# Sparse attention and a gated feed-forward on one core: another hand-written order of all steps

## The chip, the core and the metric

The kernel runs on one core of a Trainium2 chip. A core has five engines that work at the same time, each through its own queue in program order: PE (matrix products), DVE (vector), ACT (activation functions), POOL (general) and SP (which here only starts transfers). Sixteen DMA engines move data. The metric is the device time of one execution in microseconds. A profile records one execution on the same core.

## The reference

```python
# q, k, v: (4, 8, 768, 64): batch, heads, positions, head dimension
k_sum = k in blocks of 32 positions, maximum over the block       # 24 blocks
v_sum = v in blocks of 32 positions, mean over the block
scores_l = q @ k.T / 8, kept where |position difference| < 16
scores_s = q @ k_sum.T / 8 + log(32)
a = softmax(concat(scores_l, scores_s))
attn = a @ concat(v, v_sum)                                       # (4, 8, 768, 64)
x = attn.transpose(0, 2, 1, 3).reshape(3072, 512)
h = x @ w_in                                                      # (3072, 2048)
out = (h / (1 + exp(-beta * h))) @ w_out                          # (3072, 512)
```

## The kernel before, in words

The four batches go through the same stages, one after another on PE: the attention of batch b, then the products with w_in ("h", 16 column tiles of 128 by 768 tokens), then the products with w_out ("o", 6 tiles of 128 tokens by 512, each in 4 parts). Only the attention of batch 0 stands alone, ahead of everything. The attention of batch b+1 is woven into the o stage of batch b and partly into its h stage.

Attention works by head pairs: two of the eight heads, four pairs for each batch. The order of every step on every engine is written out by hand: the string ORDER (L528 to L585) is walked once (the loop at L637), and each word emits the instructions of one step into the queues of the engines concerned. A word is step.batch.pair, with a letter at the end where the engine is chosen by hand: P is POOL, D is DVE, A is ACT, S is the transfer queue of SP. A plus sign ahead of a step takes its PSUM buffer from the tag "big" (three buffers) and not from "t" (two). The steps of a pair are:

- ld.k, ld.q, ld.v load 384 KB each. They are started on SP, in the order of the string (L92, L103). Batch 0 goes to buffers of its own, later batches share five "hold" buffers.
- kc, qc cast k and q to bf16 (L98 in batches 0 and 1). kt, qt transpose them on PE (L257), ke, qe copy the result out of PSUM (L267, L272, L276).
- km takes the block maxima of k on DVE (L296), ks spreads them into the windows (L302, L303).
- vc0, vc1 cast v (L322; in later batches POOL casts the whole, and DVE's vr sorts the rows), vd makes the shifted copy of its rows (L327 and L328 as transfers, L331 and L332 as copies), vm forms the block means on PE (L347), ve takes them out (L355, L356, or L358 when they are not split in two halves), vs spreads them (L366 as a copy, L363 as a transfer).
- s0, s1 are the scores on PE. With the letter P the mask is added on PE (L395, L397) ahead of the scores (L403); later batches have L413. e0, e1 are the exponentials on ACT (L420), m0, m1 the masks on DVE (L426).
- a0, a1 are the products with v on PE (L442), n0, n1 the division by the row sums on DVE (L449, L450).
- x transposes the pair's output on PE (L462) and xe copies it out (L466). x0, x1, xe0, xe1 are halves of these. xx does the whole by one transposing transfer from SP instead (L469).

The h products of one tile (L485) contract over the four head pairs. hp does the first three pairs of a tile, hq the fourth, so that hp can start before the last pair is ready. hs is the Silu on ACT (L490). The products with w_out are at L510, their copies out of PSUM at L516 (oe), the stores at L522 (os).

The weights are loaded by POOL's queue, cast on the way: w_in in three parts wa (column tiles 0 to 3), wb (4 to 9), wc (10 to 15), w_out in two, wd (row tiles 0 to 7) and we (8 to 15). A dictionary AFTER makes some loads wait for the landing of another, to keep the transfers in a chosen order; a wait stands in the queue of the issuing engine, so what is queued behind it waits as well. ws.n (L202) divides row tile n of w_out by beta on DVE. cz, cy, cw are constants for later batches, te and tl load ACT's tables for exponential and Silu. fp.n issues n products with a buffer of zeros (L232), whose result nobody reads.

Of the kernel before, what the change touches and what calls it, by code (L numbers as in the profile page):

```python
# [11 lines left out]
def kernel(  # L12
# [505 lines left out]
    def o_store(b, ms, eng, c=slice(0, d_model)):  # L518
# [7 lines left out]


    ORDER = (  # L528
        "wm.0 sp.2 fp.14 ci.0 ld.k.0.3S on.0 ld.k.0.2S cb.0 cm.0 ld.q.0.0S lb.0 ld.v.0.0S ld.v.0.1S sp.0 "
        "ld.k.0.0S ct.0 sp.1 sp.3 ld.q.0.2S kc.0.3D ld.v.0.2S bt.0 +kt.0.3 kc.0.2A ld.v.0.3S ke.0.3D qc.0.0P "  # L530
        "ld.q.0.1S fp.3 +kt.0.2 km.0.3 ld.k.0.1S ke.0.2A fp.1 +qt.0.0 ks.0.3P qe.0.0A km.0.2 ld.q.0.3S vc1.0.0P "
        "vc0.0.0D ks.0.2P fp.6 vm.0.0 vc0.0.1A vc1.0.1P vd.0.0S ve.0.0 vd.0.1P vm.0.1P kc.0.0A ve.0.1 vs.0.0A "
        "vs.0.1D fp.2 kt.0.0 ke.0.0D qc.0.2A km.0.0 vc1.0.2P fp.6 qt.0.2 ks.0.0D qe.0.2A vc0.0.2D fp.1 s0.0.0P wa "
        "vc0.0.3A vd.0.2D s0.0.2P vc1.0.3P e0.0.0 qc.0.1D vm.0.2P wb s1.0.2P vd.0.3S e0.0.2 ve.0.2 kc.0.1D "
        "+qt.0.1 e1.0.2 +vm.0.3P wc vs.0.2D kt.0.1 s1.0.0P ke.0.1A qe.0.1D wd e1.0.0 we km.0.1 fp.1 +a0.0.0 "
        "qc.0.3P a1.0.0 n0.0.0 ks.0.1P qt.0.3 n1.0.0 ve.0.3 fp.1 x.0.0 vs.0.3D s0.0.1P qe.0.3D +a0.0.2 e0.0.1 "
        "+a1.0.2 n0.0.2 s1.0.1P n1.0.2 +a0.0.1 e1.0.1 xe.0.0D x.0.2 s1.0.3P xe.0.2A n0.0.1 +a1.0.1 e1.0.3 n1.0.1 "
# [12 lines left out]
        "qe.1.3A a1.1.0 os.0.1 o.0.2.1 kc.2.0 n0.1.1 vd.1.3S o.0.2.2 n1.1.0 kx.2.0 s1.1.2 km.1.3 xx.1.0 s0.1.2 "  # L550
        "e1.1.2 ld.v.2.1S a1.1.1 o.0.2.3 ks.1.3P n1.1.1 e0.1.2 qc.2.0 s0.1.3 m1.1.2 oe.0.2A o.0.3.0 xx.1.1 m0.1.2 "
        "e0.1.3 a1.1.2 a0.1.2 vc.2.0 n1.1.2 s1.1.3 o.0.3.1 os.0.2 e1.1.3 n0.1.2 vm.2.0 vr.2.0 tl.1 o.0.3.2 kc.2.1 "
        "ve.2.0 xx.1.2 vm.1.3 o.0.3.3 vs.2.0D o.0.4.0 qc.2.1 m1.1.3 ld.k.2.2S oe.0.3A ve.1.3 kx.2.1 o.0.4.1 "
        "m0.1.3 os.0.3 o.0.4.2 vs.1.3D vd.2.0S o.0.4.3 ke.2.0A km.2.0 a0.1.3 oe.0.4D a1.1.3 o.0.5.0 ld.q.2.2S "
        "n0.1.3 o.0.5.1 ks.2.0D os.0.4 vc.2.1 n1.1.3 x0.1.3 o.0.5.2 xe0.1.3A vr.2.1 ld.v.2.2S x1.1.3 vm.2.1 "
        "o.0.5.3 xe1.1.3D ld.k.2.3S ve.2.1 h.1.0 oe.0.5D vs.2.1D os.0.5 h.1.1 hs.1.0 vd.2.1D ld.q.2.3S kc.2.2 "
        "h.1.2 hs.1.1 km.2.1 kx.2.2 ke.2.1A h.1.3 ld.v.2.3S hs.1.2 ks.2.1D h.1.4 hs.1.3 qx.2.0 h.1.5 hs.1.4 "
        "qx.2.1 h.1.6 hs.1.5 h.1.7 hs.1.6 vc.2.2 h.1.8 hs.1.7 vr.2.2 vm.2.2 hs.1.8 h.1.9 kc.2.3 vd.2.2D ve.2.2 "
        "kx.2.3 h.1.10 hs.1.9 vs.2.2D h.1.11 hs.1.10 h.1.12 hs.1.11 km.2.2 ke.2.2A h.1.13 hs.1.12 ks.2.2D vc.2.3 "
        "h.1.14 hs.1.13 qc.2.2 vr.2.3 vm.2.3 hs.1.14 h.1.15 vd.2.3S ve.2.3 vs.2.3D qc.2.3 qx.2.2 ld.k.3.0S s1.2.0 "  # L560
        "hs.1.15 ld.q.3.0S s0.2.0 o.1.0.0 qx.2.3 ld.v.3.0S te.2 s0.2.1 ld.k.3.1S km.2.3 o.1.0.1 ld.q.3.1S e0.2.0 "
        "ke.2.3D o.1.0.2 ks.2.3D e1.2.0 o.1.0.3 m0.2.0 e0.2.1 m1.2.0 o.1.1.0 oe.1.0A m0.2.1 a0.2.0 os.1.0 s1.2.1 "
        "n0.2.0 a1.2.0 e1.2.1 o.1.1.1 n1.2.0 kc.3.0 s0.2.2 m1.2.1 xx.2.0 a0.2.1 e0.2.2 ld.v.3.1S s1.2.2 n0.2.1 "
        "o.1.1.2 kx.3.0 e1.2.2 qc.3.0 m0.2.2 a1.2.1 m1.2.2 o.1.1.3 ld.k.3.2S n1.2.1 a0.2.2 s1.2.3 oe.1.1D s0.2.3 "
        "xx.2.1 e1.2.3 o.1.2.0 n0.2.2 e0.2.3 m1.2.3 o.1.2.1 vc.3.0 tl.2 os.1.1 m0.2.3 a1.2.3 a1.2.2 vr.3.0 a0.2.3 "
        "kc.3.1 o.1.2.2 n1.2.2 vd.3.0S o.1.2.3 n1.2.3 o.1.3.0 qc.3.1 n0.2.3 xx.2.2 vm.3.0 oe.1.2D o.1.3.1 xx.2.3 "
        "ve.3.0 o.1.3.2 vs.3.0D o.1.3.3 os.1.2 o.1.4.0 oe.1.3A qx.3.1 vc.3.1 o.1.4.1 ke.3.0A km.3.0 vm.3.1 "
        "o.1.4.2 os.1.3 vr.3.1 o.1.4.3 qx.3.0 kc.3.2 vd.3.1D o.1.5.0 ks.3.0D kx.3.2 o.1.5.1 ld.q.3.2S oe.1.4D "
        "o.1.5.2 ve.3.1 os.1.4 vs.3.1D o.1.5.3 ld.v.3.2S h.2.0 oe.1.5D kx.3.1 h.2.1 hs.2.0 h.2.2 hs.2.1 os.1.5 "
        "h.2.3 hs.2.2 ld.k.3.3S h.2.4 hs.2.3 ld.q.3.3S h.2.5 hs.2.4 ld.v.3.3S h.2.6 hs.2.5 km.3.2 h.2.7 hs.2.6 "  # L570
        "ke.3.2D ks.3.2D qc.3.2 h.2.8 hs.2.7 qx.3.2 h.2.9 hs.2.8 h.2.10 hs.2.9 vc.3.2 h.2.11 hs.2.10 km.3.1 "
        "vr.3.2 vm.3.2 hs.2.11 h.2.12 vd.3.2D h.2.13 ve.3.2 hs.2.12 kc.3.3 vs.3.2D h.2.14 ke.3.1D hs.2.13 kx.3.3 "
        "ks.3.1D qc.3.3 h.2.15 hs.2.14 qx.3.3 s0.3.0 hs.2.15 s0.3.1 vc.3.3 o.2.0.0 te.3 vr.3.3 vm.3.3 o.2.0.1 "
        "vd.3.3D e0.3.1 o.2.0.2 ve.3.3 ke.3.3A o.2.0.3 vs.3.3D e0.3.0 o.2.1.0 m0.3.1 oe.2.0A km.3.3 a0.3.1 s1.3.2 "
        "os.2.0 s1.3.0 n0.3.1 e1.3.2 o.2.1.1 ks.3.3D e1.3.0 o.2.1.2 m1.3.2 m1.3.0 a1.3.2 o.2.1.3 m0.3.0 n1.3.2 "
        "a1.3.0 oe.2.1A a0.3.0 n1.3.0 o.2.2.0 os.2.1 n0.3.0 s1.3.1 s0.3.2 e1.3.1 xx.3.0 o.2.2.1 e0.3.2 m1.3.1 "
        "o.2.2.2 m0.3.2 a1.3.1 s0.3.3 n1.3.1 a0.3.2 e0.3.3 o.2.2.3 n0.3.2 xx.3.1 s1.3.3 m0.3.3 xx.3.2 o.2.3.0 "
        "e1.3.3 oe.2.2D a0.3.3 tl.3 m1.3.3 os.2.2 o.2.3.1 n0.3.3 a1.3.3 o.2.3.2 n1.3.3 o.2.3.3 xx.3.3 o.2.4.0 "
        "oe.2.3D o.2.4.1 os.2.3 o.2.4.2 o.2.4.3 o.2.5.0 oe.2.4D o.2.5.1 os.2.4 o.2.5.2 o.2.5.3 h.3.0 oe.2.5A "
        "os.2.5 h.3.1 hs.3.0 h.3.2 hs.3.1 h.3.3 hs.3.2 h.3.4 hs.3.3 h.3.5 hs.3.4 h.3.6 hs.3.5 h.3.7 hs.3.6 h.3.8 "  # L580
        "hs.3.7 h.3.9 hs.3.8 h.3.10 hs.3.9 h.3.11 hs.3.10 h.3.12 hs.3.11 h.3.13 hs.3.12 h.3.14 hs.3.13 h.3.15 "
        "hs.3.14 o.3.0.0 hs.3.15 o.3.0.1 o.3.0.2 o.3.0.3 o.3.1.0 oe.3.0A o.3.1.1 os.3.0 o.3.1.2 o.3.1.3 o.3.2.0 "
        "oe.3.1D o.3.2.1 os.3.1 o.3.2.2 o.3.2.3 o.3.3.0 oe.3.2D o.3.3.1 os.3.2 o.3.3.2 o.3.3.3 o.3.4.0 oe.3.3D "
        "o.3.4.1 os.3.3 o.3.4.2 o.3.4.3 o.3.5.0 oe.3.4A o.3.5.1 oe0.3.5 os0.3.5 os.3.4 o.3.5.2 o.3.5.3 oe1.3.5 "
        "os1.3.5 ")  # L585
# [102 lines left out]
```

## Time and profile before

| | |
|---|---|
| median of 6 runs | 231.34 us (230.16 to 234.21) |
| the profiled execution | 231.34 us |
| its span, from first to last instruction | 229.3 us |
| outside the span | 2.0 us |
| instructions | 4653 |
| busy, PE / DVE / ACT / POOL | 216.6 / 128.0 / 121.5 / 49.9 us |
| granted TensorE clock | 0.998 |
| transfers | 37.47 MB; read from HBM 27.27 MB |

The page gives busy time by engine, a map of the span in slices, the transfers, the chain of work that ended last and the costliest groups of instructions. The trace can also be asked for stretches of time, for one engine in order of time, and for waits. PE ends are modelled: a busy PE is not always a PE at its peak.

### The profile page before, as it was taken

To read this page: it belongs to the slowest core of one execution; us is meant where nothing else is said; L and a number is where in the kernel's file an instruction comes from. 1 tells how busy PE (TensorE), PEld (TensorE's weight loads), DVE (VectorE), ACT (ScalarE), POOL (GpSimd) and SP (SyncE) were. 2 spreads that over 40 slices of the span, in tenths; PEclk is the share of its full clock that TensorE was granted. 3 is DMA by queue.
4 is the path that set the end of the run, shared out by engine and by line. 5 is a ranking of instruction groups with operands and counts; after the bars stand their busy time and mean duration, and the time that the engine had idled before them with its cause. 6 is when DMAs were issued, how large, how long until landed. Compare 5 with 4: busy or idle time off the path is not lost.

```text
span 229.3 us, 4653 instructions
## 1 busy us (share of the span) xinstructions
PE 216.6 (94%) x1880; PEld 122.5 (53%) x1880; DVE 128.0 (56%) x298; ACT 121.5 (53%) x151; POOL 49.9 (22%) x76
## 2 busy tenths in 40 slices
PE   7777799999899999999999999999999999999992
PEld 3535565666456455556564455655454456654462
DVE  7789978697998976344689642353766100001111
ACT  2586276678777605667844216768554067661010
POOL 0587001250864320340243200240000000000000
PEclk9999999999999999999999999999999999999999
DMA  6999999993999799993999999993126210001212
GB/s 192 274 305 243 210 198 235 237 256 86 241 218 245 157 252 227 256 177 63 218 232 202 175 230 224 243 176 68 49 80 140 103 46 0 3 1 46 93 46 93
DMA packets 89510, 37.47 MB, mean 163 GB/s; under 512 B 78816, under 2 KB 84720, under 8 KB 89488
## 3 DMA queue, kind: packets, MB, share of 16 engines
q1 hardware_dynamic: 85728, 32.94, 64.2%
q0 software_dynamic: 3664, 4.19, 10.8%
q8 instruction: 14, 0.23, 0.4%
q14 instruction: 8, 0.07, 0.1%
q10 hardware_dynamic: 96, 0.04, 0.1%
HBM read 27.27 MB, written 6.29 MB: 146 GB/s over the span
## 4 chain that ended last, share of the span: by engine, by line
PE 83%; DVE 9%; DMA 3%; POOL 1%; issue 1%; ACT 1%; SPq 1%; DVEq 0%; ACTq 0%; POOLq 0%
PE h_ps L485 37%; PE o_ps L510 35%; PE s_ps L413 4%; PE av_ps L442 3%; DMA room_v<-in_v_dram 3%; PE vm_ps L347 2%; DVE attn L426 1%; DVE km L296 1%; DVE vt L366 1%; DVE kw L267 1%; PE px L462 1%; DVE x_nat L450 1%; POOL vt L322 1%; ACT attn L420 1%; DVE run L98 1%
## 5 line engine op out<-in xcount | busy, mean ns | idle before, releaser
L510 PE MATMUL o_ps<-w_out_sb,h_sb 128*128 128x512 bf16 (+1 forms) x400 | 88.8, 371 | 0.0
L485 PE MATMUL h_ps<-xT,w_in_sb 128*128 128x384 bf16 x512 | 85.0, 326 | 0.1
L490 ACT ACTIVATE h_sb<-h_ps,beta_sb 128x768 bf16<-128x768 f32 x64 | 57.3, 900 | 35.9 <-PE h_ps L485 35.3
L485 PEld LDWEIGHTS <-w_in_sb 128*128 128x128 bf16 x512 | 49.6, 98 | 33.1 <-issue 0.3
L510 PEld LDWEIGHTS <-h_sb 128*128 128x128 bf16 x400 | 36.7, 98 | 37.2
L516 DVE COPY o_sb<-o_ps 128x512 f32<-128x512 f32 (+1 forms) x14 | 9.1, 652 | 49.9 <-PE o_ps L510 49.8
L420 ACT ACTIVATE attn<-s_ps 128x768 bf16<-128x768 f32 x32 | 25.0, 807 | 16.6 <-PE s_ps L413 10.7
L516 ACT COPY o_sb<-o_ps 128x512 f32<-128x512 f32 x11 | 6.4, 586 | 33.3 <-PE o_ps L510 33.1
L426 DVE TENSOR_TENSOR attn<-attn,band 128x768 bf16<-128x768 bf16 x24 | 16.6, 703 | 4.5 <-ACT attn L420 3.5
L450 DVE TENSOR_TENSOR x_nat<-av_ps,r 128x384 bf16<-128x384 f32 x32 | 17.8, 558 | 1.1
L316 POOL CAST v_nat<-hold_n 128x768 bf16<-128x768 f32 x12 | 10.8, 899 | 23.0 <-DMA hold_n<-in_v_dram 15.6
L442 PEld LDWEIGHTS <-attn 128*64 128x64 bf16 x384 | 8.3, 110 | 7.9 <-issue 5.2
L248 POOL CAST qz<-hold_n 128x384 bf16<-128x384 f32 x16 | 8.4, 555 | 17.8 <-DMA hold_n<-in_q_dram 16.3
L296 DVE TENSOR_REDUCE km<-kT 128x24 bf16<-128x768 bf16 x8 | 7.6, 952 | 8.0 <-DMA kT<-k_nat 7.8
L232 PE MATMUL fill<-filler 128*128 128x384 bf16 x37 | 10.1, 403 | 2.0 <-DVE filler L636 1.2
L355 DVE COPY part<-vm_ps 32x128 f32<-32x128 f32 x15 | 4.4, 296 | 13.3 <-PE vm_ps L347 12.9
L322 DVE COPY vt<-v_nat 64x768 bf16<-64x768 bf16 x24 | 10.2, 426 | 2.4 <-POOL v_nat L316 2.2
L242 POOL CAST k_nat<-hold_n 128x768 bf16<-128x768 f32 x8 | 7.0, 880 | 19.6 <-DMA hold_n<-in_k_dram 19.1
L98 POOL CAST run<-hold_n 96x1024 bf16<-96x1024 f32 (+1 forms) x8 | 8.0, 1010 | 14.6 <-DMA hold_n<-in_k_dram 14.6
L413 PE MATMUL s_ps<-q,kw 128*128 128x128 bf16 (+2 forms) x156 | 11.0, 215 | 0.1
L442 PE MATMUL av_ps<-vt,attn 128*64 128x65 bf16 x384 | 10.8, 198 | 0.2
L128 ACT ACT_TABLE_LOAD x8 | 10.3, 1283 | 0.9 <-PEq L672 0.7
(88 smaller groups left out, 165.9 us busy)
## 6 DMA issues: line engine op xcount, KB each, us to landing
out_dram<-o_sb SPq DMA_DIRECT2D x20, 256.0 KB, 2.4
hold_n<-in_k_dram SPq DMA_DIRECT2D x12, 384.0 KB, 5.3
hold_n<-in_q_dram SPq DMA_DIRECT2D x12, 384.0 KB, 5.6
hold_n<-in_v_dram SPq DMA_DIRECT2D x12, 384.0 KB, 4.5
w_out_sb<-in_moe_w_out_dram POOLq DMA_DIRECT2D x2, 1024.0 KB, 19.3
room_k<-in_k_dram SPq DMA_DIRECT2D x4, 384.0 KB, 4.5
room_q<-in_q_dram SPq DMA_DIRECT2D x4, 384.0 KB, 5.5
room_v<-in_v_dram SPq DMA_DIRECT2D x4, 384.0 KB, 6.2
```

Of the source, the lines that this page charges most:

```text
L128: nc.scalar.activation(out=warm[:, 1:2], in_=warm[:, 0:1], func=func)
L316: nc.gpsimd.tensor_copy(out=t.rearrange("p c h d -> p h c d"), in_=f.rearrange("p (h c d) -> p h c d", h=2, d=D))
L322: copy(out=vdst(vt(b, g))[0:QT, par::2], in_=src[par * QT:(par + 1) * QT])
L413: nc.tensor.matmul(sv[:, i // NH, i % NH, :, lo:hi], window(kw, t), q2_bufs[g][:, :, t0:t0 + hi - lo], start=True, stop=True)
L420: nc.scalar.activation(out=dst, in_=src, func=ACTF.Exp, scale=scale)
L426: nc.vector.tensor_mul(out=a, in0=a, in1=band[:, u * nch:(u + 1) * nch, None].to_broadcast([P, nch, 2, QT]))
L442: nc.tensor.matmul(o[par * QT:(par + 1) * QT, mi * VW + c.start:mi * VW + c.stop], a[:, i, h] if b else a[:, h, i], v_t[:, u * nch + i, c] ...
L450: nc.vector.tensor_mul(out=x[:, u * NH:(u + 1) * NH], in0=ov.rearrange("p m (h e) -> p m h e", e=VH)[:, :, :, 0:D], in1=r[:, :, :, None].t ...
L485: nc.tensor.matmul(big[:, kk, 0:MG], w_in_sb[:, ki, ni * P:(ni + 1) * P], xT[b][:, ki, kk * MG:(kk + 1) * MG], start=(ki == 0), stop=(ki = ...
L490: nc.scalar.activation(out=h_bufs[(b, ni // 8)][:, ni % 8, :].rearrange("p (k m) -> p k m", k=2), in_=h_open[(b, ni)][:, :, 0:MG], func=AC ...
L510: nc.tensor.matmul(o_ps[(b, ms)][:, c], h_bufs[(b, ni // 8)][:, ni % 8, ms * P:(ms + 1) * P], w_out_sb[:, ni, c], start=(ni == 0), stop=(n ...
L516: copy(out=o_out[(b, ms)][:, c], in_=o_ps[(b, ms)][:, c])
```

## The change

The kernel's functions stay as they are. ORDER and AFTER are replaced. What differs most:

- Batch 0: the pairs are loaded and computed in the order 1, 0, 2, 3 (before: k of pair 3 and 2, then q and v of pair 0, then mixed, with k and q of pair 1 and 3 last).
- Batch 0: several steps have another engine. All ke and qe are on ACT (two of each were on DVE). vs is on POOL twice and a transfer once (before: three times DVE, once ACT). xe of pair 1 is replaced by the transposing transfer xx.0.1. kc of one pair is on POOL. ks of pairs 0 and 1 is on DVE. Three vm are not split.
- 25 filler products in place of 37.
- wa waits for q of pair 3 (before: v of pair 3). In batch 1, k and q of pair 0 wait for wc, and v of pair 0 for wd; k of pair 1 no longer waits for we.
- Batch 1: the first three h tiles are begun on three of the four pairs (hp.1.0 to hp.1.2, hq.1.0 to hq.1.2) in place of h.1.0 to h.1.2. So it was done in batch 0 already.
- Steps of batches 1 to 3 change places by a few words and some change their engine.

The core of the diff (the lines up to the first products with w_in, the start of h in batch 1, and AFTER):

```diff
-        "wm.0 sp.2 fp.14 ci.0 ld.k.0.3S on.0 ld.k.0.2S cb.0 cm.0 ld.q.0.0S lb.0 ld.v.0.0S ld.v.0.1S sp.0 "
-        "ld.k.0.0S ct.0 sp.1 sp.3 ld.q.0.2S kc.0.3D ld.v.0.2S bt.0 +kt.0.3 kc.0.2A ld.v.0.3S ke.0.3D qc.0.0P "
-        "ld.q.0.1S fp.3 +kt.0.2 km.0.3 ld.k.0.1S ke.0.2A fp.1 +qt.0.0 ks.0.3P qe.0.0A km.0.2 ld.q.0.3S vc1.0.0P "
...
+        "wm.0 sp.0 fp.14 ci.0 ld.k.0.1S sp.2 sp.1 sp.3 cb.0 ld.v.0.1S cm.0 ld.k.0.0S lb.0 ld.q.0.1S ld.v.0.0S "
+        "on.0 ld.v.0.2S ct.0 ld.q.0.0S kc.0.1D ld.k.0.2S bt.0 kt.0.1 ke.0.1A vc0.0.1P ld.k.0.3S vc1.0.1A km.0.1 "
+        "ld.v.0.3S kc.0.0A fp.6 +vm.0.1 vd.0.1P ks.0.1D ld.q.0.2S ld.q.0.3S qc.0.1A ve.0.1 +kt.0.0 ke.0.0A "
+        "vs.0.1P qt.0.1 vc1.0.0D vc0.0.0A km.0.0 qe.0.1A fp.3 vm.0.0P vd.0.0S vc0.0.2P ks.0.0D s0.0.1P ve.0.0 "
+        "s1.0.1P vc1.0.2D qc.0.0P e0.0.1 +vm.0.2 vd.0.2S vs.0.0P e1.0.1 +qt.0.0 ve.0.2 kc.0.2A a0.0.1 vs.0.2S "
+        "+a1.0.1 kc.0.3P n0.0.1 qe.0.0A +kt.0.2 n1.0.1 kt.0.3 ke.0.2A s1.0.0P vc1.0.3P vc0.0.3D xx.0.1 ke.0.3A "
+        "s0.0.0P km.0.2 qc.0.2P e1.0.0 vm.0.3 km.0.3 ks.0.2P e0.0.0 +qt.0.2 wa a1.0.0 ve.0.3 qe.0.2A qc.0.3D "
+        "a0.0.0 ks.0.3P n1.0.0 +qt.0.3 s1.0.2P wb qe.0.3A vd.0.3D s0.0.2P wc e1.0.2 n0.0.0 s1.0.3P wd e0.0.2 "
+        "vs.0.3D +a1.0.2 we e1.0.3 x.0.0 n1.0.2 +a0.0.2 xe.0.0A s0.0.3P n0.0.2 +a1.0.3 e0.0.3 x.0.2 n1.0.3 tl.0 "
+        "fp.1 a0.0.3 xe.0.2D +x1.0.3 n0.0.3 fp.1 hp.0.0 xe1.0.3A x0.0.3 hp.0.1 xe0.0.3A hq.0.0 hq.0.1 hs.0.0 "
...
+        "ws.4 ld.k.1.1S ws.7 ke.1.0A ld.q.1.1S ws.5 qc.1.0P h.0.11 ws.3 ld.v.1.1S hs.0.10 km.1.0 qt.1.0 ws.0 "
+        "hs.0.11 h.0.12 ws.2 ws.1 qe.1.0A ks.1.0D h.0.13 hs.0.12 h.0.14 ws.11 ld.k.1.2S ws.10 hs.0.13 ws.14 "
+        "h.0.15 ws.13 hs.0.14 ws.15 ws.9 vc.1.0 s0.1.0 ws.8 hs.0.15 s1.1.0 ws.12 ld.q.1.2S vm.1.0 vr.1.0 kc.1.1P "
...
-        "o.0.5.3 xe1.1.3D ld.k.2.3S ve.2.1 h.1.0 oe.0.5D vs.2.1D os.0.5 h.1.1 hs.1.0 vd.2.1D ld.q.2.3S kc.2.2 "
+        "xe0.1.3A x1.1.3 ks.2.0D vm.2.0 oe.0.5A ld.k.2.3S hp.1.0 vc.2.1 xe1.1.3D ve.2.0 hq.1.0 vs.2.0D vm.2.1 "
+        "hs.1.0 hp.1.1 os.0.5 vr.2.1 hq.1.1 hp.1.2 kc.2.2 ve.2.1 ld.q.2.3S hs.1.1 vs.2.1D hq.1.2 kx.2.2 h.1.3 "
...
-    AFTER = {"wa": "ld.v.0.3", "wb": "ld.q.0.2", "wc": "ld.q.0.3", "wd": "ld.q.0.3", "we": "ld.q.0.3", "ld.k.1.0": "wc", "ld.q.1.0": "wd", "ld.v.1.0": "wb", "ld.k.1.1": "we", "ld.q.1.1": "wb", "ld.v.1.1": "wc", "ld.k.1.2": "wd", "ld.q.1.2": "wb", "ld.v.1.2": "we", "ld.q.1.3": "wc", "ld.v.1.3": "we"}
+    AFTER = {"wa": "ld.q.0.3", "wb": "ld.q.0.2", "wc": "ld.k.0.2", "wd": "ld.k.0.3", "we": "ld.q.0.2", "ld.k.1.0": "wc", "ld.q.1.0": "wc", "ld.v.1.0": "wd", "ld.v.1.1": "wb", "ld.k.1.2": "we", "ld.v.1.2": "wb", "ld.q.1.3": "wc", "ld.v.1.3": "wc"}
```

## The prediction

> **What bounds the kernel now.** I read three views: first the page's busy times, then a table of stretches cut where PE changes stage, then each engine in order of time for the first 33 us. The page's first line and five rows of the table (stretch, its length, busy time and instructions of PE, weight loads, DVE, ACT, POOL, clock, DMA share, GB/s):
>
> ```profile
> PE 216.6 (94%) x1880; PEld 122.5 (53%) x1880; DVE 128.0 (56%) x298; ACT 121.5 (53%) x151; POOL 49.9 (22%) x76
> ```
> ```profile
> 0.00:32.67 32.67, 25.16 (x387) 15.78 (x388) 27.31 (x73) 18.77 (x22) 13.52 (x24) 1.00 1.06 238
> 32.67:55.72 23.05, 23.05 (x172) 14.46 (x172) 17.92 (x43) 16.08 (x20) 5.91 (x8) 1.00 0.90 203
> 55.72:86.56 30.84, 29.77 (x305) 15.71 (x303) 27.99 (x57) 18.67 (x27) 15.02 (x21) 1.00 1.00 221
> 108.97:135.49 26.52, 26.52 (x245) 13.39 (x243) 19.53 (x46) 11.12 (x16) 6.55 (x9) 1.00 1.14 208
> 204.43:225.22 20.79, 20.75 (x112) 10.77 (x110) 2.50 (x4) 2.07 (x3) 0.00 (x0) 1.00 0.15 57
> ```
>
> From the first h product at 32.67 to the last product at 225.22 PE is full, but for 1.07 us in the o stage of batch 0 (29.77 of 30.84). That part of 192.55 us can give back 1.07 us and hardly more. What is left is the 32.67 us ahead of it: there DVE is busy for 27.31 us and PE partly with fillers. The last of the twelve loads of batch 0 (q of pair 3, started at 13.81, 5.3 us to landing) has landed at 19.1, and h begins 13.6 us later. In DVE's order of time, DVE works without a real gap from 13.3 to 25.5. So the prologue waits for DVE, and then for what hangs on it:
>
> ```profile
> 19.70 0.98 DVE run L98
> 20.69 0.81 DVE vt L366
> 21.53 0.96 DVE q L272
> 22.52 0.95 DVE km L296
> ...
> 23.61 0.56 DVE x_nat L450
> ...
> 24.92 0.51 PE px L462 x6
> 25.43 0.33 PE s_ps L395 x2
> ...
> 32.67 1.14 PE h_ps L485 x6
> ```
>
> This is the chain that ended last: casts, copies out of PSUM and maxima, one behind another on DVE, then the scores of pairs 1 and 3, which could begin only behind them.
>
> **Part by part: the prologue's engines.** Durations are rows of this trace. DVE loses two ke and two qe (4 x 0.96), one cast of k (0.97), two vs (0.81 + 0.55), the second half of three ve in place of one (2 x 0.30) and two xe (0.55 + 0.36). It gains one ks (0.58 + 0.77) and one v cast (0.54). Sum: -7.7 + 1.9 = -5.8 us of 27.3. ACT gains two ke and two qe (4 x 0.80) and half an xe (0.46), and loses one vs (1.47): +2.2 on 18.8. POOL gains a cast of k (1.08) and two vs and loses a v cast (0.82). No row shows vs on POOL. The nearest is the shifted copy there, 1.35 us for 1408 elements, so 1.48 for 1536. Below: not under 1.35; above: 1.9, if DVE holds it up as it does with its neighbours. I take 1.48, +3.2 us on 13.5. Each engine stays under 22 us, so none is full any more.
>
> **The prologue's path.** Loads are the same twelve of 384 KB, only permuted; I give them the landing slots of before: k1 4.3, v1 5.7, k0 7.4, q1 8.8, v0 10.4, v2 11.8, q0 12.6, k2 13.8, k3 15.2, v3 16.5, q2 17.9, q3 19.1. All twelve stand ahead of the small transfers on SP, as before. The gain lies in what is ready when they land. Pair 1 is complete at 8.8: ACT copies its q out of PSUM by 12.7 (behind the copies of v0, landed at 10.4), its scores run from there to 14.2, its exponentials end near 14.9. Then ACT works through kc.0.2 (1.04), qe.0.0, ke.0.2, ke.0.3 (0.80 each), both exponentials of pair 0 (0.81 each) and qe.0.2 (0.80): 5.9 us, to 20.8. PE meanwhile waits for the shifted v of pair 0: the same transfer was started at 15.03 and took 5.9, so 20.9. From there PE's queue is a0.0 and a1.0 (0.31 each), qt.3 (0.33), s1.2 (0.81), s0.2 (0.73), s1.3 (0.81), a1.2 (0.31), x.0 (0.51), a0.2 (0.31), s0.3 (0.73), a1.3 (0.31): 5.5 us, to 26.4. Then n1.3 (0.70) and xe.2 on DVE (0.55): h at 27.65. ACT's six copies and exponentials behind 20.8 end at 25.6, so it isn't later. Some 17 hand-overs between engines at 0.045 us (the "issue" pieces of the chain are 0.03 to 0.06) make 0.75: **h at 28.4, 4.3 us earlier**.
>
> What this rests on: *wa*, now behind q3, is started at 19.5 on POOL and not at 15.46. It stands ahead of ks.0.3 there, whose reader s1.3 comes at 23, two us later. Its landing took 7.8 us, of which 3.6 beside the last loads; 19.5 plus 4.2 or 7.8 gives 23.7 to 27.3, hidden. At 11.3, the slowest w_in part, it is 30.8 and costs 2.4. *xx.0.1* takes the place of 0.51 on PE and 0.80 on ACT; it starts at about 18, behind the shifted copies on SP, such transfers took 2.7 to 5.1, and its reader comes at 28.4: nothing, with 5 us of cover. *vs of pair 2* as a transfer starts near 17, and at the 5.9 of its neighbour lands by 23 with its reader at 24.1: nothing to +1. SP has six small transfers behind the twelve loads, where it had four, at 0.5 to 1.3 us of its queue; the next load behind them, k of batch 1, waits for wc anyway.
>
> **The fillers.** Twelve fewer; at full rate 12 x 0.163 = 2 us of PE that has idle time there. But the first rows show what they are for:
>
> ```profile
> 1.16 4.66 PE L232 MATMUL fill<-filler 128*128 128x384 bf16 x14 [1.16 <-DVE filler L636]
> ```
>
> 333 ns each; later ones start 163 ns apart. The Trainium skill ("TensorE: Matmul & The Clock Gate", Part 1) says that PE's clock is halved after an idle window of about 3.4 us, and Part 4 that transposes don't count as work. That speaks against removing fillers. The thinnest stretch of before, 19.90 to 23.30, has 1.96 us of PE busy in 3.40, some 0.5 of it transposes, and the rate held. In the new order the thinnest is about 8.3 to 11.7: vm 0.5, kt 0.35, qt 0.33, three fillers 0.5, so 1.7, and 1.0 without transposes. By the row nothing is lost, since it is near what held. By the rule, read strictly, it isn't idle either, but the margin is thin. Nothing is gained below zero. If the clock did fall and stayed down until h: 14 fillers show 4.66 us at half rate, so 2.3 us lost at the start of h, and the four scores behind 20.9 (3.1 us) would take twice as long. I take zero and keep +5.4.
>
> **The o stage of batch 0.** h of batch 0 keeps 23.05, so o begins at 51.5. Weight loads don't move 4 us earlier: the transfers are full in both (DMA share above 0.9), and they start 0.5 to 1 us later. *we* landed at 43.0 with three loads of batch 1 started ahead; now it is six. At 1.4 us for a load (twelve from 2.2 to 19.1) that would be up to 4.2 more, 48.2, if all go ahead of it. The skill ("DMA: Bandwidth & Descriptors", Queues, rings and completion order) says an engine takes queues in turn, by packets. Then loads beyond the ones already in contention add nothing: 44. The trace has both queues progressing together from 37 to 43 (two loads landed in 6.2 and 7.0, we with them), which is nearer the second; I take 46. Behind *we* on DVE stand eight ws (ten took 4.67, so 3.8) and vr.1.0 (0.7): 50.5, where before had 53.4. From there to the first product of h in batch 1 it was 33.2 us, in which DVE was nearly full (27.99 of 30.84 in the stage). The same path gives 83.7; PE's own path is 28.4 + 23.05 + 30.84 = 82.3; DVE's 2.9 us of idle in the stage can bring the first down to 80.9. I take 82.8, 3.75 us before the 86.56 of now. That is a new wait of 0.5 us, beside the old 1.07.
>
> hp for batch 1 covers a copy of 0.36 to 0.48 us, where the trace shows no gap of PE: nothing, from +0.2 (two more switches of group; four o products take 0.97 and not 0.86 after one) to -0.2. The later stages, with PE full, have moved words only: 0, up to +0.5. Tail unchanged, 4.08.
>
> Sum: 231.34 - 3.75 = **227.6**. The profiled execution is the median, so nothing is to be corrected.
>
> **The rivals.**
> *No new wait:* h at 27.65 and PE full in the o stage: -5.0 - 1.07 gives 225.2. For it: DVE has slack there of 2.9 us. Against it: DVE is at 91% in that stage, the highest of all.
> *w_out late:* we at 48.2, so vr.1.0 at 52.7, h of batch 1 at 85.9 by the old path, 83.0 with DVE's idle gone: 227.8 to 230.7. For it: six loads ahead. Against it: the two queues that advanced together.
> *The clock (slower):* PE falls to half rate between 8.3 and 11.7 and is still there when h starts: +5.4, 233.0. It decides from 3.75 us lost. For it: twelve fillers gone, transposes that don't count. Against it: the stretch of before that held with 1.96 of 3.40.
>
> **How the numbers follow.** A measurement of this kernel can tell about 0.3% (0.7 us) from no change. Forecast, 226.2 to 229: 0.63. No new wait: 0.14. w_out late: 0.15 faster, 0.03 within 0.3%. The clock: 0.05 slower. So faster 0.92, same 0.03, slower 0.05. The range 225.6 to 229.9 leaves out about half of the first rival, a third of the second and the third.
>
> **What would show it.** h at 28 to 29, with DVE under 23 us busy before it; scores of pair 1 near 13; wa landed by 27; fillers and scores between 10 and 28 at 163 ns spacing, else the clock; we at 44 to 48 and the o stage of batch 0 at 31 to 31.5; stages behind it within 0.3 us each. I am wrong if h waits for wa or a small transfer, or if the o stage takes back over 2 us.

## The result and the profile after

Before, 230.97 us in the median of all runs beside those of the new kernel; after, 230.2 us. The ratio is 0.9937 with a 95% interval of 0.9919 to 0.9954: 1.5 us faster, where 3.7 were forecast. (The two medians, of all runs, lie only 0.8 us apart; the ratio is taken from the fast runs alone, those within 1.5% of each kernel's fastest.) 230.2 lies above the range, whose upper end was 229.9. The profiled execution of after took 230.1 us, its span 228.1 (before 229.3). Busy times of the page first:

```profile
PE 214.8 (94%) x1862; PEld 121.5 (53%) x1862; DVE 118.3 (52%) x285; ACT 126.5 (55%) x160; POOL 52.9 (23%) x74
```

Then the table of stretches of after, cut at the same changes of stage as before:

```profile
0.00:27.89 27.89, 22.47 (x370) 14.51 (x371) 21.60 (x65) 19.33 (x25) 16.51 (x24) 1.00 0.98 218
27.89:53.03 25.14, 22.86 (x166) 14.17 (x164) 13.68 (x41) 17.96 (x23) 2.72 (x3) 1.00 1.18 226
53.03:85.41 32.38, 30.37 (x308) 16.23 (x304) 28.57 (x56) 19.14 (x28) 16.24 (x23) 1.00 1.15 224
108.03:134.68 26.65, 26.65 (x248) 13.34 (x245) 19.60 (x44) 13.00 (x20) 6.61 (x9) 1.00 1.12 208
203.56:224.52 20.96, 20.93 (x114) 10.85 (x111) 1.81 (x3) 2.66 (x4) 0.00 (x0) 1.00 0.15 55
```

Line by line: the prologue is 4.78 us shorter (27.89 for 32.67), with DVE at 21.60 us for 27.31. Then 2.09 are given back in the h stage of batch 0 (25.14 for 23.05; before, PE was full there, now 2.28 are idle), and 1.54 in the o stage (32.38 for 30.84). That leaves 1.15. The later stages are as they were: from the first product of h in batch 1 to the end of the span it is 142.7 us in both. So the question is what lengthened two stages in which the change does little. The waits of PE in the h stage of after have one line (total, times, longest):

```profile
PE pk L257 <- POOL run L98: 2.3, 1, 2.3
```

That is the transpose of k of batch 1's first pair (kt.1.0), waiting for its cast. The chain that ended last in after leads back from it (start, us, what):

```profile
12.74 8.36 DMA room_q<-in_q_dram
21.09 0.31 issue
21.40 0.89 POOL w_in_sb L210
...
23.23 0.69 POOL w_in_sb L210
23.91 11.99 DMA w_in_sb<-in_moe_w_in_dram
35.90 0.02 issue
35.92 6.33 DMA hold_n<-in_k_dram
...
42.37 1.08 POOL run L98
43.45 0.05 issue
43.49 0.51 PE pk L257 x8
```

Read upward: the cast waits for k, k is gated on wc (AFTER), wc lands at 35.9 (before: 30.7), because it is started behind wa, which waits for q of pair 3, landed at 21.09. In before the three parts of w_in were started at 15.46, 17.12 and 19.43, and k of batch 1 on SP at 30.75 (idle time ahead and its releaser in brackets):

```profile
15.46 0.90 POOL L210 DMA_DIRECT2D w_in_sb<-in_moe_w_in_dram  x1 [0.56 <-DMA room_v<-in_v_dram]
17.12 0.88 POOL L210 DMA_DIRECT2D w_in_sb<-in_moe_w_in_dram  x1
19.43 0.74 POOL L210 DMA_DIRECT2D w_in_sb<-in_moe_w_in_dram  x1 [1.43 <-DMA room_q<-in_q_dram]
30.75 0.34 SPq L92 DMA_DIRECT2D hold_n<-in_k_dram  x1
```

POOL's queue in after shows that the gate is only the last of it:

```profile
16.84 0.82 POOL L322 CAST vt<-room_v 64x768 bf16<-64x768 f32 x1
19.70 0.82 POOL L98 CAST run<-room_q 128x768 bf16<-128x768 f32 x1 [2.04 <-ACT attn L420]
20.47 0.42 POOL L302 COPY kw<-km 128x288 bf16<-128x288 bf16 x1
20.84 0.20 POOL L303 COPY kw<-kw 128x32 bf16<-128x32 bf16 x1
21.40 0.89 POOL L210 DMA_DIRECT2D w_in_sb<-in_moe_w_in_dram  x1 [0.35 <-DMA room_q<-in_q_dram]
```

POOL stood 2.04 us ahead of the cast of q of pair 2, reached wa at 21.04, and the wait for q of pair 3 held it 0.35 more. The view names an exponential as what ended the 2.04 us, but q of pair 2 landed at the same moment, 19.55 (started at 10.23, 9.3 us), and it was the load that held the cast: in two later kernels with the same prologue the same cast is released by the load (e2), or runs before that exponential has begun, its load having landed earlier (e6, exponential at 17.96):

```profile
19.00 0.82 POOL L98 CAST run<-room_q 128x768 bf16<-128x768 f32 x1 [1.43 <-DMA room_q<-in_q_dram]
17.61 1.03 POOL L98 CAST run<-room_q 128x768 bf16<-128x768 f32 x1
```

So both delays are late landings of the last two loads of batch 0, and they vary between executions: with this prologue wa starts at 21.40 here, at 20.69 in e2, 20.36 in e4 and 19.85 in e6. Meanwhile the transfers moved half as much or less. The same three stretches of 2 us, first before, then after; the last two columns are DMA share and GB/s:

```profile
18.00:20.00 2.00, 1.91 (x46) 1.25 (x40) 1.87 (x6) 1.53 (x3) 0.57 (x1) 1.00 1.21 238
20.00:22.00 2.00, 1.15 (x28) 0.94 (x27) 1.94 (x3) 0.73 (x2) 2.00 (x3) 1.00 1.18 217
22.00:24.00 2.00, 1.40 (x32) 0.96 (x31) 1.93 (x4) 0.78 (x2) 1.30 (x4) 1.00 1.18 215
```
```profile
18.00:20.00 2.00, 1.46 (x26) 0.91 (x25) 1.97 (x4) 1.60 (x3) 0.30 (x1) 1.00 0.56 119
20.00:22.00 2.00, 1.09 (x32) 0.91 (x33) 0.83 (x3) 0.80 (x1) 1.65 (x4) 1.00 1.28 107
22.00:24.00 2.00, 2.00 (x41) 1.34 (x42) 1.89 (x6) 1.53 (x3) 2.00 (x5) 1.00 0.49 50
```

By 24 before had moved 0.8 MB more (670 less 276 GB/s, times 2 us). Yet the share of the whole prologue reads 0.98: an average hides such a hole. The share of 1.28 in after's middle row, at only 107 GB/s, goes with the transposing transfer xx.0.1, under way from 18.69 to 22.65: in e3, which leaves it out, the share reads 0.04 from 19 to 20 and 0.00 from 20 to 21.

### The profile page after: what moved, and what is told of

It is laid out like the page before. It is cut to its first block, busy times and chain, and to the rows that moved or that the text cites. A ratio compares the mean times of both kernels' runs of the same rounds, so it can differ in the third digit from the quotient of the medians.

```text
span 228.1 us, 4619 instructions
## 1 busy us (share of the span) xinstructions
PE 214.8 (94%) x1862; PEld 121.5 (53%) x1862; DVE 118.3 (52%) x285; ACT 126.5 (55%) x160; POOL 52.9 (23%) x74
## 4 chain that ended last, share of the span: by engine, by line
PE 73%; DMA 12%; DVE 6%; SPq 5%; POOL 2%; issue 1%; POOLq 0%
PE o_ps L510 33%; PE h_ps L485 31%; DMA w_in_sb<-in_moe_w_in_dram 5%; DMA room_q<-in_q_dram 4%; SPq L92 4%; PE s_ps L413 3%; DMA hold_n<-in_k_dram 3%; PE av_ps L442 3%; DVE attn L426 2%; SPq L103 2%; PE vm_ps L347 1%; DVE vt L366 1%; DVE vt L322 1%; DVE km L296 1%; POOL w_in_sb L210 1%
## 5 line engine op out<-in xcount | busy, mean ns | idle before, releaser
L490 ACT ACTIVATE h_sb<-h_ps,beta_sb 128x768 bf16<-128x768 f32 x64 | 57.3, 900 | 26.7 <-PE h_ps L485 26.5
L516 DVE COPY o_sb<-o_ps 128x512 f32<-128x512 f32 (+1 forms) x9 | 5.7, 632 | 43.9 <-PE o_ps L510 43.9
L516 ACT COPY o_sb<-o_ps 128x512 f32<-128x512 f32 x16 | 9.4, 585 | 34.4 <-PE o_ps L510 21.1
L316 POOL CAST v_nat<-hold_n 128x768 bf16<-128x768 f32 x12 | 10.1, 845 | 36.5 <-DMA hold_n<-in_v_dram 23.6
L322 DVE COPY vt<-v_nat 64x768 bf16<-64x768 bf16 x24 | 11.6, 485 | 12.9 <-POOL v_nat L316 12.7
L426 DVE TENSOR_TENSOR attn<-attn,band 128x768 bf16<-128x768 bf16 x24 | 15.2, 641 | 4.6 <-ACT attn L420 4.3
L248 POOL CAST qz<-hold_n 128x384 bf16<-128x384 f32 x16 | 8.9, 582 | 16.7 <-DMA q<-qz 9.4
L98 POOL CAST run<-hold_n 96x1024 bf16<-96x1024 f32 (+1 forms) x8 | 8.0, 1007 | 19.6 <-DMA hold_n<-in_k_dram 17.8
L442 PE MATMUL av_ps<-vt,attn 128*64 128x65 bf16 x384 | 11.3, 198 | 1.2 <-DMA vt<-vt 1.1
L413 PEld LDWEIGHTS <-kw 128*128 128x128 bf16 x156 | 9.7, 98 | 3.8 <-DVE x_nat L450 1.1
L242 POOL CAST k_nat<-hold_n 128x768 bf16<-128x768 f32 x8 | 7.7, 962 | 15.9 <-DMA hold_n<-in_k_dram 10.3
L267 ACT COPY kw<-pk 128x768 bf16<-128x768 bf16 x7 | 5.6, 796 | 8.5 <-PE pk L257 8.5
```

Of the source, the lines that this page charges most:

```text
L316: nc.gpsimd.tensor_copy(out=t.rearrange("p c h d -> p h c d"), in_=f.rearrange("p (h c d) -> p h c d", h=2, d=D))
L322: copy(out=vdst(vt(b, g))[0:QT, par::2], in_=src[par * QT:(par + 1) * QT])
L413: nc.tensor.matmul(sv[:, i // NH, i % NH, :, lo:hi], window(kw, t), q2_bufs[g][:, :, t0:t0 + hi - lo], start=True, stop=True)
L426: nc.vector.tensor_mul(out=a, in0=a, in1=band[:, u * nch:(u + 1) * nch, None].to_broadcast([P, nch, 2, QT]))
L442: nc.tensor.matmul(o[par * QT:(par + 1) * QT, mi * VW + c.start:mi * VW + c.stop], a[:, i, h] if b else a[:, h, i], v_t[:, u * nch + i, c] ...
L490: nc.scalar.activation(out=h_bufs[(b, ni // 8)][:, ni % 8, :].rearrange("p (k m) -> p k m", k=2), in_=h_open[(b, ni)][:, :, 0:MG], func=AC ...
```

## The experiments

Theory A: the weights start too late, and what hangs on them (k of batch 1, w_out) eats the gain. Its rivals have other letters in the expectations. Each ratio is to before, from runs on the same chip. "h", "o" and "h of batch 1" are the starts of the first products in PE's order of time in one profiled execution; kernels with the same prologue (after, e2, e4, e6) differ there by 1 us, so a single difference below that says little. Where the profiled execution lies far from the median (both are in the table), its stage times stand for that execution and not for the kernel; of e1 and e9 mainly the reasons for waits are read.

| kernel | ratio (95%) | median, profiled (us) | h | o | h of batch 1 | h stage | o stage |
|---|---|---|---|---|---|---|---|
| before | 1 | 231.0, 231.3 | 32.67 | 55.72 | 86.56 | 23.05 | 30.84 |
| after | 0.9937 (0.9919 to 0.9954) | 230.2, 230.1 | 27.89 | 53.03 | 85.41 | 25.14 | 32.38 |
| e1 early weights | 0.9895 (0.9835 to 0.9954) | 229.9, 234.4 | 30.01 | 59.08 | 89.92 | 29.07 | 30.84 |
| e2 kt later | 0.9922 (0.9894 to 0.9951) | 229.6, 229.4 | 27.19 | 52.31 | 84.31 | 25.12 | 32.00 |
| e3 fewer small | 0.9959 (0.9935 to 0.9982) | 230.3, 230.7 | 27.69 | 53.32 | 86.14 | 25.63 | 32.82 |
| e4 whole h | 0.9922 (0.9885 to 0.9958) | 229.9, 229.9 | 26.92 | 53.61 | 85.28 | 26.69 | 31.67 |
| e5 = e1 + e3 | 0.9838 (0.9790 to 0.9885) | 227.4, 228.7 | 28.95 | 51.64 | 84.17 | 22.69 | 32.53 |
| e6 k after wb | 1.0001 (0.9969 to 1.0034) | 231.1, 229.0 | 27.20 | 51.26 | 84.56 | 24.06 | 33.30 |
| e7 = e5 + e6 | 0.9903 (0.9869 to 0.9937) | 228.7, 228.6 | 28.02 | 50.70 | 83.95 | 22.68 | 33.25 |
| e8 no small | 1.0090 (1.0070 to 1.0111) | 233.0, 231.4 | 30.55 | 54.95 | 86.59 | 24.40 | 31.64 |
| e9 late gate in before | 1.0022 (0.9998 to 1.0046) | 231.9, 234.9 | 33.10 | 56.15 | 89.42 | 23.05 | 33.27 |
| e10 = e5 + copies | 0.9971 (0.9948 to 0.9995) | 230.4, 230.5 | 31.52 | 54.21 | 85.69 | 22.69 | 31.48 |
| e11 = e5, no masks | 0.9803 (0.9780 to 0.9826) | 226.2, 225.8 | 28.21 | 50.90 | 81.31 | 22.69 | 30.41 |
| e12 = e5, vs moved | 0.9846 (0.9819 to 0.9874) | 227.3, 228.0 | 29.43 | 52.12 | 83.49 | 22.69 | 31.37 |
| e13 = e5, DVE relieved | 0.9839 (0.9810 to 0.9868) | 227.0, 227.5 | 28.39 | 51.08 | 83.03 | 22.69 | 31.95 |

**e1: weights early.** wa and wb stand behind vc1.0.3 on POOL and wait for v of pair 3, as wa did before.

```diff
- ... s1.0.0P vc1.0.3P vc0.0.3D xx.0.1 ... +qt.0.2 wa a1.0.0 ... s1.0.2P wb qe.0.3A
+ ... s1.0.0P vc1.0.3P wa wb vc0.0.3D xx.0.1 ... +qt.0.2 a1.0.0 ... s1.0.2P qe.0.3A
- AFTER = {"wa": "ld.q.0.3", "wb": "ld.q.0.2", ...
+ AFTER = {"wa": "ld.v.0.3", "wb": "ld.v.0.3", ...
```

> The new order, but wa and wb stand on POOL right behind the last v cast of batch 0 and wait for v of pair 3 (landed 16.7), as wa did before, and no longer for q of pair 3 (21.1). Theory A (the late start of the weights gave the gain back: wa at 21.4 and not 15.5, with the transfers half empty from 18 to 24): wc lands at 32 to 33 and not 35.9, k of batch 1 at 38 to 39, PE's 2.3 us wait for its cast is gone, the o stage of batch 0 shrinks by about 1; 226.5 to 227.5 us, 1.2 to 1.6% below the new order. Theory B (transfers are full, an earlier weight only pushes q of pairs 2 and 3 back): q of pair 3 lands at 22 to 23, h starts at 29 to 30, total within 0.5 us of the new order (229.5 to 230.5).

Measured: wa starts at 17.19, but a new wait stands at the head of h. PE's order of time in e1:

```profile
30.01 0.33 PE L485 MATMUL h_ps<-xT,w_in_sb 128*128 128x384 bf16 x1
33.90 1.76 PE L485 MATMUL h_ps<-xT,w_in_sb 128*128 128x384 bf16 x5 [3.56 <-DMA xT<-x_nat]
```

This is xx.0.1, the transposing transfer. It took 15.4 us beside the weights in this execution; in after 4.0. Late in the wait the granted clock falls, and it reads 0.50 from 33 to 39, which lengthens this h stage further. The late weights of the new order also clear the way for the transfer. So A is not answered by e1 alone: the transfer has to go too. Whether the wait stands in every execution of e1 is not shown; one of its six took 227.41 us, as little as e5.

**e2: the waiting transpose later.** kt.1.0 goes behind h.0.11, qt.1.0 behind h.0.12.

```diff
- ... ld.v.1.0S kt.1.0 hs.0.9 h.0.10 ... h.0.11 ws.3 ld.v.1.1S hs.0.10 km.1.0 qt.1.0 ... h.0.12
+ ... ld.v.1.0S hs.0.9 h.0.10 ... h.0.11 kt.1.0 ws.3 ld.v.1.1S hs.0.10 ke.1.0A km.1.0 ... h.0.12 qt.1.0
```

> The new order, but the transposes of k of batch 1's first pair stand two h tiles later on PE (behind tile 11 and not 9), with q's behind tile 12. Loads untouched. Theory A (late transfers): the 2.3 us wait on PE at 41 disappears, but the attention of batch 1 is no earlier, so most of it comes back in the o stage as waits for its loads; 0 to 0.8 us below the new order. Theory C (only the place on PE is wrong): 2.3 us below the new order, about 227.5 to 228.

Measured: the wait for k is gone, and one for v of batch 1 stands in its place, so h takes 25.12 as in after. PE's waits from h to the o stage in e2:

```profile
PE vm_ps L347 <- POOL v_nat L316: 1.8, 1, 1.8
```

It isn't the place of kt.1.0: v of that pair comes too late as well. Time and interval agree with after.

**e3: fewer small transfers.** vs of pair 2 goes to DVE, and xx.0.1 to PE and DVE (x, xe).

```diff
- ... a0.0.1 vs.0.2S ... vc0.0.3D xx.0.1 ke.0.3A
+ ... a0.0.1 vs.0.2D ... vc0.0.3D x.0.1 xe.0.1D ke.0.3A
```

> The new order, but vs of pair 2 is a copy on DVE again and the output of pair 1 is transposed on PE and copied out on DVE, not by a transposing transfer: two small transfers fewer between 18 and 23. Theory D (the small transfers hold back q of pairs 2 and 3 and with them wa): q of pair 3 lands at 19 to 20 and not 21.1, wa starts by 20.5, wc lands by 34.5; 0.8 to 1.5 us below the new order. Theory A (the empty stretch is the gate's alone): q of pair 3 lands within 0.5 of 21.1, total within 0.7 us of the new order.

Measured: wa at 20.33, still late, and PE waits 2.78 us for k of batch 1; no gain. These two transfers aren't the loss.

**e4: the hp part undone.** h.1.0 to h.1.2 whole again, without hp and hq.

```diff
- ... hp.1.0 ... hq.1.0 ... hp.1.1 ... hq.1.1 hp.1.2 ... hq.1.2
+ ... h.1.0 ... h.1.1 ... h.1.2
```

> The new order, but the first three h tiles of batch 1 are whole again (h.1.0 to h.1.2), not begun on three of the four pairs. All theories of mine: PE waits for the copy of the last half of pair 3 where now it does pairs 0 to 2; 0 to 0.7 us above the new order. If this part mattered for the gain, it would be over 1 us above.

Measured: 0.9922, inside after's interval. This part is worth nothing that can be measured. (The h stage of batch 0, in which e4 and after have the same steps, reads 26.69 because behind the wait for k, 2.15 us, the clock fell to 0.50 from 43 to 46.)

**e5: e1's and e3's edits together.** The weights are early, and two transfers are gone, xx.0.1 and vs of pair 2.

> As the run with the weights early (wa and wb behind the last v cast, waiting for v of pair 3), but the output of pair 1 is transposed on PE and copied out on DVE, and vs of pair 2 is a copy on DVE: no small transfer is left that stands behind the weights and that h waits for (there the transposing transfer took 15.4 us beside the weights, 4.0 in the new order, and h waited for it). Theory A: h at 27.5 to 29, wc lands at 33 to 34.5, k of batch 1 by 40.5, PE's wait for its transposition under 0.5; 1.5 to 3 us below the new order, 227 to 228.5. Theory B (the transfers are the bound in sum): wc lands no earlier than 35 or h no earlier than 29.5; within 0.7 us of the new order.

Measured: 227.4 us. Stages of e5:

```profile
0.00:28.95 28.95, 22.62 (x376) 14.85 (x376) 22.57 (x67) 20.11 (x26) 16.53 (x24) 1.00 1.00 231
28.95:51.64 22.69, 22.69 (x166) 14.26 (x164) 13.28 (x42) 17.17 (x21) 3.87 (x5) 1.00 1.18 218
51.64:84.17 32.53, 30.59 (x307) 16.05 (x304) 28.86 (x55) 19.12 (x28) 15.03 (x22) 1.00 1.06 223
```

PE is full through h again (22.69 of 22.69). Two pairs of kernels bear on A: with the transfer kept, late weights give 0.9937 and early ones 0.9895, in overlapping intervals; without it, late ones give 0.9959 and early ones 0.9838, and those two intervals are apart. The second pair settles it, and e12 and e13 repeat it on another chip (0.9846, 0.9839). Early weights are worth 1.2% (2.8 us) once nothing else stands in their traffic. A small part of that is PE's clock: e5 kept it in all six executions, e3 in ten of 22, and those ten (mean clock 0.997 or more) average 229.8 us, e5 227.3. In all six kernels with early weights and x.0.1 on PE (e5, e7, e10 to e13) the h stage is 22.7; in those of the new order with late ones 24.1 to 26.7.

**e6 and e7: the gate of k.** In e6, k and q of pair 0 of batch 1 wait for wb and v for wc; e7 adds e5.

```diff
- "ld.k.1.0": "wc", "ld.q.1.0": "wc", "ld.v.1.0": "wd"
+ "ld.k.1.0": "wb", "ld.q.1.0": "wb", "ld.v.1.0": "wc"
```

> The new order, but k and q of batch 1's first pair wait for wb and not wc, its v for wc and not wd. Nothing else. Theory E (the gate between weights and batch 1's loads is in the wrong place: wc, needed at 41, and wd, needed at 52, are let ahead of k, needed at 41): k lands at 38 to 39.5 and not 42.3, wc at 38 to 39.5, still ahead of its reader; the 2.3 us wait on PE is gone, v of the first pair lands by 48; 2 to 3.5 us below the new order. Theory A (only an earlier start of the weights can help, what is given to k is taken from wc and we): PE waits for wc or for w_out instead; 0 to 1 us below the new order.

> Both edits: weights early with pair 1 transposed on PE, and batch 1's first loads behind wb and wc. If the two gates are separate prices (A and E both hold): h at 27.5 to 29, no wait over 0.5 us in the h stage, o stage of batch 0 at 31 to 31.5; 226 to 227.5 us. If they are one and the same price: no more than 0.5 us below the better of the two.

Measured: in e6 k starts at 31.3 and its wait is gone, but others come up (1.30 us for vm's input, 0.49 for the divided w_out, 1.21 ahead of the products with v), and the time is that of before. e7 begins o earliest of all and its median is 1.3 us above e5's. Both fit a delay that is only passed on to the transfers behind the gate; nothing shows the gate misplaced. The profiled execution of e6 is its shortest, 2 us under the median, so what the others waited for is not seen.

**e8: no small transfers at all.** e3, and the shifted copies of pairs 0 and 2 on DVE (vd.0.0D, vd.0.2D for S).

> The new order with its gates, but no small transfer at all before the weights: both shifted copies of v that were transfers are copies on DVE, vs of pair 2 too, pair 1's output is transposed on PE. Theory D (small transfers hold back the last loads): q of pair 3 lands by 19.3 and not at 20 to 21, wa starts by 19.8, wc lands by 34.3, 1 us or more below the new order. Theory A (the gate: weights start only when the last load is complete, and the transfers run empty meanwhile): q of pair 3 lands no earlier than 19.7, the stretch from 18 to 22 stays under 150 GB/s, wc at 34.5 to 36; within 0.8 us of the new order.

Measured: slower than before. q of pair 3 landed at 19.4; with four small transfers it landed at 19.2 to 21.2 (e3, e5, e7), with all six at 19.6 to 21.1 (after, e2, e4, e6), so a price of the small transfers does not stand clear of that scatter. With the shifted copies on DVE, PE stood still for 1.93 us behind a cast there and then ran at half rate, and wa started only at 23.18, since POOL waited 2.85 us for a maximum on DVE. PE's clock (the third column from the right) in the stretches of e8:

```profile
13.00:15.00 2.00, 0.24 (x9) 0.11 (x2) 1.90 (x5) 0.98 (x3) 1.05 (x2) 1.00 1.14 277
16.00:22.00 6.00, 6.00 (x88) 4.46 (x85) 4.88 (x11) 3.12 (x5) 3.34 (x4) 0.50 0.31 108
```

In the second row PE reads busy for all of the 6 us, at half rate. This is the rival of the clock, in another kernel, and in every execution of it: the mean clock of all 22 is 0.985 or less.

**e9: the late gate in before.** wa waits for q of pair 3 and stands behind vc1.0.3.

> The kernel before, with one thing taken over from the new order: wa waits for q of pair 3 (19.1) and not for v of pair 3 (15.2); on POOL it stands one v cast later so that this cast doesn't wait. Theory A: the same empty stretch shows here, behind 18, wc lands at 34 to 35.5 and not 30.7, k of batch 1 at 40 to 42; as h starts at 32.7 here, PE waits little in the h stage, more in the o stage: 0.5 to 2 us above before. If the gate doesn't matter (transfers are the bound in sum): within 0.4 us of before.

Measured: 1.0022 (0.9998 to 1.0046). The hole is there (45 GB/s from 18 to 20), wa starts at 18.87 and k of batch 1 at 32.9 in place of 30.75. The h stage keeps its 23.05, and the price is at most 1 us, with h beginning at 33. A late gate is cheap for an order whose h begins late; but it was also less late here, since in after wc landed 3 us later still.

**e10: e5 with e8's copies.**

> As the run with weights early and pair 1 transposed on PE, and the two shifted copies of v on DVE as well: nothing small is in flight beside the loads and the weights. Theory A with both parts: h at 27.5 to 29, wc at 31 to 33, no wait over 0.5 us in the h stage; 226.3 to 227.8 us, at or up to 1 us below that run (0.984 of before). If the copies cost more on DVE than the transfers cost (DVE has 1.4 us more): h at 29.5 or later, 228 to 229.

Measured: 230.4, 3 us above e5; again a gap of 1.93 us, then the clock at 0.50 from 17 to 23, and h at 31.52. Those shifted copies are better as transfers.

**e11 and e13: DVE in the o stage.** e11 is e5 without the eight masks of batch 1, so the local scores of that batch stay unmasked. e13 is e5 with three copies of DVE moved to ACT (ke.1.1A, oe.0.4A, vs.1.2A).

> The run with weights early and pair 1 transposed on PE (0.984 of before), less the eight masks of batch 1 on DVE (0.5 to 1.1 us each); the local scores of batch 1 are left unmasked, so this leaves out a part of the computation. Theory F (DVE's chain of work sets the end of batch 0's o stage): the first h product of batch 1 comes at 82.5 or sooner and not at 84.2, the total falls by 1.2 to 2.5 us. Theory G (batch 1's loads set it): 83.8 to 84.5, the total within 0.7 us.

> The run with weights early and pair 1 transposed on PE, with three steps of batch 0's o stage on ACT and not on DVE: the copy of k of pair 1 (0.97), the spread of v sums of pair 2 (0.6 to 1), one copy of an output tile (0.65). Everything is computed. Theory F: the first h product of batch 1 comes 0.7 to 1.5 us sooner (82.7 to 83.5), and the total falls as much, to 226 to 226.8. Theory G: within 0.5 us of that run, or above it where ACT comes late.

Measured: e11's o stage takes 30.41, with DVE at 21.47 for 28.86:

```profile
50.90:81.31 30.41, 29.30 (x301) 15.86 (x304) 21.47 (x47) 19.05 (x28) 14.16 (x22) 1.00 1.11 230
```

That is the shortest of all, 1 us below the next with early weights (e12, 31.37). In these profiles h of batch 1 begins 2.9 us ahead of e5's, 0.7 of which come from the prologue; but e5's is its longest execution and e11's its shortest, and the medians differ by 1.1 us only, in overlapping intervals. e12 and e13 ran on the same chip as e11: its median is 1.0 and 0.7 us below theirs, and all five of its times lie below all six of e12's. So the masks on DVE do cost time in this stage, 0.7 to 1.1 us of the whole. Without them each pair also has one step less between its exponential and its products, and the run doesn't tell that from DVE's load. e13 is within the noise of e5: moving three copies is not enough to be seen.

**e12: e5 with vs of pair 2 kept as a transfer.**

> The run with weights early and pair 1 transposed on PE, but vs of pair 2 is the transfer of the new order again. If only the transposing transfer stood in the way of early weights: within 0.7 us of that run (0.981 to 0.987 of before), h at 28 to 29. If small plain transfers behind the weights are held up as well: vs lands after 25.5 (it took 7.5 us once), h at 29.5 or later, 0.99 or above.

Measured: 0.9846, the same as e5; vs took 4.7 us. Of the two transfers that e3 removes, only the transposing one can stand against early weights. That it does rests on the one profile of e1.

## Why the prediction failed

**The prologue: right.** h was forecast at 28.4 and begins at 27.89; DVE was to be under 23 us and is at 21.60. The scores of pair 1 begin at 11.79 (forecast near 13), the products with the shifted v of pair 0 at 21.42 (forecast 20.9), behind its transfer as forecast. vs on POOL took 1.85 and 1.68, inside its bounds of 1.35 and 1.9, but above the 1.48 taken. POOL has 16.51 us of work, near the sum (13.5 + 3.2).

**The failed step: "Weight loads don't move 4 us earlier: the transfers are full in both (DMA share above 0.9), and they start 0.5 to 1 us later."** They start 4 to 6 us later: wa 21.40 for 15.46, wb 23.18 for 17.12, and wc lands at 35.9 for 30.7. The error is in the working and not only in the estimate. With its own 19.5 for wa, that load alone is 4 us late, and wc behind wa and ks.0.3 on POOL can't start at 19.43 as before. The argument that full transfers make the start of one unimportant used an average, and the hole from 18 to 24 lies just where the gate stands. To this come 1.9 us between 19.5 and 21.40, from the landings of q of pair 2 and 3 at 19.55 and 21.09 (forecast 17.9 and 19.1). Most of that varies from execution to execution (wa starts at 19.85 in e6), and what delays these loads is not known: the small transfers, called free, are a candidate, but e8 doesn't bear it out.

**"h of batch 0 keeps 23.05": failed in consequence.** The prediction noted that k of batch 1 waits for wc, and drew from it only that SP's queue isn't held up. It didn't follow k to its reader in the h stage. There PE waits 2.28 us for it, as the chain shows. Early weights take the wait away (e5); another place of the reader only trades it for a wait for v (e2).

**The o stage: too small.** 31.3 were forecast (51.5 to 82.8), 32.38 measured. With PE's start at 53.03 the sum closes: -0.5 in the prologue, +2.1 in h, +1.1 in o, so 82.8 + 2.7 = 85.5, and 85.41 is measured. The direction (DVE limits the stage) was right, but not by the path that was given for it, from *we* through the ws on DVE: *we* landed at 49.4 and not at 46, the eight ws behind it ended at 51.6, and the chain comes to DVE only at 55.31, from PE. It runs along DVE to 70.7:

```profile
55.31 0.97 DVE kw L267
56.27 0.02 issue
56.30 0.95 DVE km L296
57.25 0.68 DVE attn L426
...
59.25 1.24 DVE vt L366
...
62.24 1.09 DVE attn L426
...
63.62 1.10 DVE vt L322
64.71 0.03 issue
64.74 0.95 DVE km L296
```

Copies, maxima and masks (L426) stand one behind another. e5 begins o 1.4 us ahead of after and takes 0.15 longer for it; e7 begins 2.3 ahead and takes 0.9 longer. e11 shows that the masks on DVE are a part of what the stage takes. Why it takes 1.1 us more than forecast stays open: DVE's work in it, 28.57 us, is only 0.6 above before's, and e13's three steps fewer were not enough to be seen.

**xx.0.1 "nothing, with 5 us of cover": right by luck, through the other error.** It took 4.0 us beside half-empty transfers. With the weights started as early as in e1, where it took 15.4, h waited 3.56 us for it in the one execution that was profiled.

**Rivals.** The clock stayed at 1.00 in the profiled execution of after; in the stretch from 8.3 to 11.7 that the prediction doubted, PE was busy for 2.46 us of 3.40. It doesn't stay there in every execution: of 37 of after, 12 have a mean clock of 0.997 or more and average 229.2 us, the other 25 230.4. Before has the same scatter (of its 137 beside the experiments, 42 such average 230.8, the other 95 231.5). At the high clock the two kernels lie 1.6 us apart, so the clock doesn't explain the missing 2 us. e8 and e10 show what it costs when it falls in the prologue.

"w_out late" named a landing of *we* at 48.2, near the measured 49.4, but for another reason: *we* was started 4.7 us later than before (25.85 for 21.13) and took 23.5 us for 21.9, so the six loads ahead of it cost it 1.6 us at most. PE did not wait for w_out in after's o stage; k of batch 1 bound first. That the rival's range of 227.8 to 230.7 holds the measured time is luck. With e5's early weights the forecast time is there, 227.4 for 227.6, though its o stage takes 32.53 us for the 31.3 forecast.

## What to carry to other kernels

When a transfer is gated, write down its start, landing and first reader before and after, for it and for all that is gated on it in turn; a DMA share averaged over the stage says nothing of the hole in front of a gate. A prologue that ends earlier needs its successors' data earlier by the same amount; a late gate that costs the old order at most 1 us (e9) can then cost most of the gain. A releaser that a view names should be checked against what else came at the same moment, best in a second kernel with the same steps. An edit costed at nothing because a cover is there should be costed again for the case in which another step of the same sum moves.

## What the hardware showed

- A transposing transfer took 4.0 us beside half-empty transfers (after, from 18.69; the eleven later ones of that profile took 2.7 to 4.7) and 15.4 beside the weight loads of POOL's queue (e1, one execution). The plain small transfer next to it (vs of pair 2) took 7.5 there, 4.3 in after, and 4.7 beside early weights in e12.
- The granted clock did not follow the length of one gap on PE. It fell to 0.50 after a gap of 1.93 us (e8, e10), after one of 2.15 (e4, at 40) and in e12 with no gap over 0.8 us since the first product; it stayed at 1.00 after 2.28 us (after, at 41) and 2.78 us (e3, at 41). The idle window of about 3.4 us, cited in the prediction from the Trainium skill ("TensorE: Matmul & The Clock Gate", Part 1), is longer than all of these gaps, so a gap kept below it did not keep the clock. What decides between these cases is open. The rows of e12, then of after:

```profile
15.00:21.00 6.00, 6.00 (x88) 4.46 (x85) 3.14 (x8) 3.23 (x5) 4.77 (x6) 0.50 0.92 243
```
```profile
42.00:44.00 2.00, 0.51 (x9) 0.46 (x10) 1.81 (x4) 0.15 (x1) 1.07 (x1) 1.00 1.16 270
```

- The spread copy (vs, 32x1536) took 1.68 and 1.85 us on POOL and 1.47 on ACT (before). On DVE it took 0.55 to 2.18 in the profile of after alone, and what stretches it there was not tested.
